# Four one-bank buffers instead of two two-bank buffers for the second product of an attention and MLP kernel

## The chip, the core and the metric

The kernel runs on one core of a Trainium2 chip, as one launch. The metric is the device time of that launch in microseconds (us). Five engines work side by side, each through its own queue in order: TensorE (PE, its weight loads PEld), VectorE (DVE), ScalarE (ACT), GpSimd (POOL), and SyncE (SP), which here issues all DMAs. Results of PE land in PSUM, which has eight banks; a bank holds 512 float32 values in each of 128 partitions.

## The reference

Causal attention by blocks of 64 over 8 batches, 8 heads, 576 positions and head size 64, and behind it a layer norm and an MLP with a residual:

```python
scores = scale * np.matmul(q, k.transpose(0, 1, 3, 2))
scores = np.where(block_i >= block_j, scores, -1000000000.0)
attn = np.exp(scores - np.max(scores, axis=-1, keepdims=True))
attn = attn / (np.sum(attn, axis=-1, keepdims=True) + 1e-09)
x = np.matmul(attn, v)            # then to (8, 576, 512)
...
xn = (x - mu) / np.sqrt(var + 1e-06) * g_ln
ch = np.maximum(xn @ w_ch1, 0.0) @ w_ch2      # 512 -> 2048 -> 512
return x + ch
```

## The kernel before

All work is recorded first as tasks of a plan (`Plan`): each task has an engine (or a choice of engines), an estimated cost, a priority, and buffers that it reads and writes (`Buf`). `Plan.run` walks through an estimated time and gives each engine the ready task of lowest priority number, and this order is the order of the instructions in the engine's queue. A buffer that is made by `kind` takes a slot when its first task is placed and gives it back when its last one ends in that estimate. The waits between engines are not written by hand: a layer below derives them from which instruction touches which tile, so the plan's opinion on when a buffer is free sets the order, and the tile sets the wait.

Attention goes over 32 pairs of heads. `pair` computes scores on PE into PSUM (`scores1` into one-bank buffers `s1`, `scores0` into two buffers `s` of two banks each), `soften` takes them out on DVE and ACT, PE turns the result (`tr`), multiplies it with v (`o`), and DVE turns that and stores it (`xd`). PSUM is divided in two kinds: the tag `tr` has four one-bank slots (`tr`, `s1`, `o`, and later `p`), the tag `s` has two two-bank slots (`s`, and later `y`).

The MLP takes the 36 tiles of 128 rows in six rounds of six. `norm_tiles` loads two tiles at a time (`x<-xd`, L612), scales them (L621), takes their statistics (L630, POOL's L648 to L651), normalises (L656, L659), turns them on DVE (`xnt`, L661) and through DRAM (`xw`, L665, and back as `xt`, L669). `operands` makes from `xt` the seven operands `xm` of a Strassen product, each as a high and a low part (L218, L686, L697). Of round n+1 all this runs beside the products of round n.

In each round there are eight groups. `products` computes the hidden units of a group with seven products `p` of six matmuls each (L789); ACT and DVE take them out (L797, L802) and make the ReLU in two parts, `h` (L808, L809). `second` is the second matrix product, one group later: for each of the six tiles of the round a **y block** of six matmuls of 512 columns (L852) goes into one PSUM bank, and DVE adds that bank to the running sum of the tile in SBUF, `ya` (L861). In PE's queue the steps of a group stand as p, y, p, y, p, p, y, p, y, p, y, y, p, by the priorities in `second` and `products`: called in the text the first to sixth y block of a group.

Two two-bank buffers, `yb2`, are made once and are held through the whole MLP; block number m uses half m modulo 4 of the four halves. `owner` remembers which block used a half last, and the plan makes a block wait for the sum that read the block four before it:

```python
yb, old = yb2[at_y // 2], owner.get(at_y)
hold = 512 * (at_y % 2)
...
add("PE", 6 * (512 / 2400 + MMO), go, ..., w=[part, *([old] if old else [])], alloc=[yb], ...)
```

Of the kernel before, what the change touches and what calls it, by code (L numbers as in the profile page):

```python
# [9 lines left out]
F32 = mybir.dt.float32  # L10
# [6 lines left out]
PSUM = bass.MemoryType.PSUM  # L17

P = 128
# [6 lines left out]
MMO = .0134  # L26
# [30 lines left out]
class Plan:  # L57
# [5 lines left out]
    def add(self, eng, cost=None, fn=None, r=(), w=(), prio=0.0, size=0, alloc=(), mode=128):  # L63
        k = Task(eng if isinstance(eng, dict) else {eng: (cost, fn)}, prio, size)
        k.mode = mode
        before = {}
        for x in r:
            before.update(dict.fromkeys(x.writers))
        for x in w:
            before.update(dict.fromkeys(x.readers))  # L70
        for x in r:
            x.readers.append(k)
        for x in w:
            x.writers.append(k)
        for x in before:
            x.next.append(k)
        k.left = len(before)
        k.uses = list(dict.fromkeys(x.root for x in (*r, *w, *alloc)))
        for x in k.uses:
            x.users += 1  # L80
        k.allocs = [x for x in dict.fromkeys(x.root for x in (*w, *alloc)) if x.make]
        self.tasks.append(k)
        return k
# [88 lines left out]
def dve(n):  # L172
    return .07 + n / 960
# [10 lines left out]
def attn_mlp_kernel(ctx: ExitStack, tc: tile.TileContext, qk, qk0, v, v0, w1, w2, g, out):  # L184
# [8 lines left out]
    nc = tc.nc  # L193
    NPAIR, _, _, S = qk.shape
# [8 lines left out]
    psum = ctx.enter_context(tc.tile_pool(name="psum", bufs=1, space=PSUM))  # L203
    odd = ctx.enter_context(tc.tile_pool(name="odd", bufs=1))
    plan = Plan()
    add = plan.add
# [15 lines left out]
    def kind(name, shape, dtype, bufs, space=None, tag=None, most=None):  # L222

        tag = tag or name
        plan.free.setdefault(tag, bufs)
        own = (tag, "of " + name) if most else (tag,)
        if most:
            plan.free["of " + name] = most

        def make():  # L230
            return (space or sb).tile(shape, dtype, name=name, tag=tag, bufs=bufs)

        def new():
            x = Buf(own, make)
            if space is not dram and name not in ("tr", "s1", "o"):
                x.after, last[name] = [y for y in (last.get(name),) if y], x
            return x
        return new


    new_s, new_y2 = (kind(n, [P, 1024], F32, 2, psum, "s") for n in ("s", "y"))
    steps = {}
    new_tr, new_s1, new_o, new_p = (kind(n, [P, 512], F32, 4, psum, "tr") for n in ("tr", "s1", "o", "p"))

# [52 lines left out]
    def load(nbytes, fn, **kw):  # L297
        add("SP", .6, fn, size=nbytes, **kw)
# [3 lines left out]
    w2b, w1b = {}, {}  # L302

    def decode(j, second, prio, gate):
        n = 512
        wrb, magb, sgnb = new_word(), new_mag(), new_sgn()
# [48 lines left out]
    def pe(at, phase, *args, **kw):  # L355
        steps.setdefault((at, phase), []).append(add("PE", *args, **kw))

    ends, big_of, batch_sums = {}, {}, {}

    def pair(k):  # L360
        b, c = k // 4, k % 4
        prio = 100 + 10 * k
        step = [0]

        def pr():
            step[0] += 1
            return prio + .05 * step[0]
# [23 lines left out]
        def soften(p, s, nm, at, i, h, cols):  # L391

            n = cols.stop - cols.start
            low, x, m = Buf(parent=p), Buf(parent=p), Buf(parent=nm)
            hide = never[:, 576 - n:576] if h else never[:, 512:512 + n]
            add("DVE", dve(n) + .01, lambda: nc.vector.tensor_tensor_reduce(  # L396
                out=p.t[:, part(i, h)], in0=s.t[:, cols], in1=hide, scale=-0.125, scalar=3e38, op0=ALU.add, op1=ALU.min,
                accum_out=nm.t[:, at:at + 1]), r=[s], w=[low, m], prio=pr())
            add("ACT", act(n, True) + .14, lambda: nc.scalar.activation(  # L399
                out=p.t[:, part(i, h)], in_=p.t[:, part(i, h)], func=AF.Exp, bias=nm.t[:, at:at + 1], scale=-1.0,  # L400
                accum_out=totals[:, i - 1, h:h + 1]), r=[low, m], w=[x, sums], prio=pr())
            return x
# [43 lines left out]
        done = [[], []]  # L446
        for h, s in enumerate(sab):
            for n, (i, cols) in enumerate(((4, slice(0, 576)), (3, slice(576, 1024)))):
                done[h].append(soften(pab, s, nm, 2 * h + n, i, h, cols))
        pt0 = big_of[k, 1] = new_pt0()  # L450
        got = []

        for h in range(2):
            for i in (4, 3):
# [4 lines left out]
                else:  # L459
# [5 lines left out]
                     r=[o], w=[x], prio=pr())  # L465
# [9 lines left out]
        for h in range(2):  # L475
# [12 lines left out]
            r=[v_sb, *got], w=[part_o[1]], alloc=[ot], prio=pr(), mode=1)  # L488
# [86 lines left out]
    for k in range(NPAIR):  # L575
        pair(k)
        if k % 8 == 3:
            first(k // 8)
    plan.chain([x for at in sorted(steps) for x in steps[at]])

    n = 0
    for j in range(NJ):
        for second in (False, True):
            decode(j, second, 100 + 10 * (D_0 + D_1 * n), [ends[min(int(D_0 + D_1 * n) - 3, NPAIR - 1)]])
            n += 1
# [244 lines left out]
        return {k: (hs[k], v) for k, v in done.items()}  # L830

    acc = {}
    yb2, owner, turn_y = [new_y2(), new_y2()], {}, [0]

    def second(n, gp, hs, base):

        for pair_, (s0, s1) in enumerate(((3, 4), (5, 0), (1, 2))):
            for z, s in enumerate((s0, s1)):
                at_y = turn_y[0] % 4
                turn_y[0] += 1  # L840
                yb, old = yb2[at_y // 2], owner.get(at_y)
                hold = 512 * (at_y % 2)
                t, h, at = ROUND * n + s, s // HALF_R, s % HALF_R * P
                part = owner[at_y] = Buf(parent=yb)

                def go(hold=hold, h=h, at=at, yb=yb):
                    y = yb.t[:, hold:hold + 512]
                    for i in range(2):
                        j = 2 * gp + i
                        x, (wh, wl) = hs[i, h][0], w2s[j // 4]  # L850
                        for e, (l, w) in enumerate(((0, wh), (0, wl), (1, wh))):
                            nc.tensor.matmul(y, x.t[:, l, at:at + P], w.t[:, j % 4], start=i == e == 0, stop=i == 1 and e == 2)  # L852
                add("PE", 6 * (512 / 2400 + MMO), go, r=[*hs[0, h][1], *hs[1, h][1], *w2b[2 * gp], *w2b[2 * gp + 1]], w=[part, *([old] if old else [])],
                    alloc=[yb], prio=base + (7, 21, 37, 51, 65, 75)[2 * pair_ + z])
                if gp == 0:
                    ya = new_ya()
                    load(P * 2048, lambda t=t, ya=ya: nc.sync.dma_start(out=ya.t, in_=xrow[t].t), r=[xparts_t[t]], w=[ya], prio=4)
                    acc[t] = ya, ya
                ya, was_ = acc[t]
                now = Buf(parent=ya)  # L860
                add("DVE", dve(512), lambda hold=hold, yb=yb, ya=ya: nc.vector.tensor_add(  # L861
                    ya.t, yb.t[:, hold:hold + 512], ya.t), r=[part, was_], w=[now], prio=1)
                acc[t] = ya, now
                if gp == GROUPS - 1:
                    load(P * 2048, lambda t=t, ya=ya: nc.sync.dma_start(out=out[t], in_=ya.t), r=[now], w=[], prio=2)
# [3 lines left out]
    for n in range(ROUNDS):  # L869
        for q in range(HALF_R):  # L870
            norm_tiles(n, q, 100 + 10 * LN_0 + q if n == 0 else END + 2 * n - 10, gate)
        operands(n, 100 + 10 * LN_0 + 3 if n == 0 else 2)
        for gp in range(GROUPS):
            base = 1e6 + 100 * (GROUPS * n + gp)
            hs = products(n, gp, base)
            if gp == 0:
                gate = hs[0, 0][1]
            if before:
                second(*before, base)
            before = n, gp, hs  # L880
# [5 lines left out]
def _run_one(arrays):  # L886
    import numpy as np
    import concourse.bacc as bacc
    from concourse.bass_utils import run_bass_kernel_spmd

    nc = bacc.Bacc("TRN2", target_bir_lowering=False, num_devices=1, dynamic_dma_scratch_size=1024)
    args = {n: nc.dram_tensor(n, a.shape, mybir.dt.from_np(a.dtype), kind="ExternalInput").ap()
            for n, a in arrays.items()}
    for n in ("w1", "w2"):
        args[n] = args[n].bitcast(I32)
    args["out"] = nc.dram_tensor("out_t", (36, P, 512), F32, kind="ExternalOutput").ap()
    with tile.TileContext(nc) as tc:
        attn_mlp_kernel(tc, *args.values())
    r = run_bass_kernel_spmd(nc, [arrays], core_ids=[0])
    return np.asarray(r.results[0]["out_t"])  # L900
# [37 lines left out]
```

## Time and profile before

| what | value |
|---|---|
| median of 3 runs | 1136.12 us (1132.82 to 1141.36) |
| the profiled execution | 1135.29 us |
| its span, first to last instruction | 1133.5 us |
| TensorE clock granted over the span | 0.992 of full speed |
| PE busy | 1075.6 us, 95% of the span |
| DVE busy | 802.6 us, 71% |
| ACT busy | 463.1 us, 41% |
| POOL busy | 270.3 us, 24% |

The profile comes from one execution of its own, 1135.29 us long; 1.8 us of it lie outside the span. A matmul is shown with an end that is modelled and reaches into the next one, so PE's busy time is not its work at full pace, and a stretch in which PE lost time may still show it as busy. The first y block starts 333.9 us after the start of the span, the last sum at 1129.6 us; what lies between is the MLP, what lies ahead is attention, with the first groups of the MLP woven in from 317.5 us on.

### The profile page before, as it was taken

Reading aid. Unit: us, or ns where it says so; the run is one execution under the profiler, and the core shown is the slowest. Engines: PE = TensorE matmul, PEld = TensorE weight load, DVE = VectorE, ACT = ScalarE, POOL = GpSimd, SP = SyncE. Lnnn points to the kernel's source line nnn. Section 1 sums busy time; section 2 is a strip of 40 time slices with the busy share of each in tenths; the row PEclk is TensorE's granted clock in tenths of the full one; section 3 lists DMA queues with packets and bytes.
Section 4 is the critical chain, followed back from the end, with each engine's and each line's share of the span. In section 5 each row is a group of like instructions: output and inputs, shape, how many; then the busy total and the mean of one; then the engine's idle time right before and its main releaser. Section 6 shows DMA issues by size and latency. Waiting matters only on the chain.

```text
span 1133.5 us, 18643 instructions
## 1 busy us (share of the span) xinstructions
PE 1075.6 (95%) x6576; PEld 903.7 (80%) x6576; DVE 802.6 (71%) x1801; ACT 463.1 (41%) x1152; POOL 270.3 (24%) x426
## 2 busy tenths in 40 slices
PE   9999998999988898899999999999999899999998
PEld 6777666777777787788888888887888788888887
DVE  5878987888798888666676565866667666754544
ACT  6778878898853332212132122322223122322221
POOL 0013725322366642112221121212201122100000
PEclk9999999999999999999999999999999999999999
DMA  5559786956587746767637765387645776363311
GB/s 177 156 164 264 228 238 233 268 206 213 190 312 248 228 142 213 220 176 193 182 125 241 190 191 167 114 240 205 177 149 178 207 197 173 137 211 123 125 71 56
DMA packets 232173, 213.31 MB, mean 188 GB/s; under 512 B 158736, under 2 KB 187408, under 8 KB 225936
## 3 DMA queue, kind: packets, MB, share of 16 engines
q1 hardware_dynamic: 232080, 212.12, 61.2%
q8 instruction: 52, 0.85, 0.3%
q14 instruction: 41, 0.34, 0.1%
HBM read 155.45 MB, written 56.62 MB: 187 GB/s over the span
## 4 chain that ended last, share of the span: by engine, by line
PE 59%; DVE 19%; DMA 8%; SPq 5%; ACT 3%; issue 3%; POOL 2%; DVEq 0%; POOLq 0%; ACTq 0%
PE y L852 26%; PE p L789 19%; PE s L381 4%; PE tr L408 4%; PE o L418 4%; DVE ya L861 3%; DMA x<-xd 3%; DMA wr<-w 3%; SPq L612 2%; PE o L414 2%; DMA ya<-xrow 2%; DVE h L809 2%; ACT pu L399 1%; DVE pab L396 1%; DVE xm L697 1%
## 5 line engine op out<-in xcount | busy, mean ns | idle before, releaser
L852 PE MATMUL y<-w2h,h 128*128 128x512 f32 x1152 | 402.4, 398 | 31.4 <-DVE ya L861 31.2
L861 DVE TENSOR_TENSOR ya<-y,ya 128x512 f32<-128x512 f32 x288 | 196.8, 685 | 193.7 <-PE y L852 187.7
L852 PEld LDWEIGHTS y<-w2h,h 128*128 128x128 f32 x1152 | 217.1, 188 | 85.3 <-DVE ya L861 42.3
L789 PE MATMUL p<-xm,wa 128*128 128x384 f32 x1152 | 226.8, 339 | 3.3 <-DVE xm L697 1.7
L852 PE MATMUL y<-w2l,h 128*128 128x512 f32 x576 | 227.5, 395 | 0.0
L789 PEld LDWEIGHTS p<-xm,wa 128*128 128x128 f32 x1152 | 207.2, 190 | 12.1 <-DVE xm L218 2.0
L808 ACT ACTIVATE h<-t 128x384 fp32r<-128x384 f32 x144 | 75.6, 525 | 328.6 <-DVE t L802 325.5
L789 PE MATMUL p<-xm,wb 128*128 128x384 f32 x864 | 177.1, 340 | 2.8 <-ACT t L797 2.4
L789 PEld LDWEIGHTS p<-xm,wb 128*128 128x128 f32 x864 | 156.5, 189 | 15.2 <-ACT t L797 2.7
L852 PEld LDWEIGHTS y<-w2l,h 128*128 128x128 f32 x576 | 108.8, 189 | 15.8
L797 ACT COPY t<-p 128x384 f32<-128x384 f32 x144 | 68.5, 476 | 112.0 <-PE p L789 105.7
L802 DVE TENSOR_TENSOR t<-p,t 128x384 f32<-128x384 f32 x144 | 79.2, 550 | 26.7 <-PE p L789 26.5
L381 PE MATMUL s<-raw 64*128 64x320 f32 (+4 forms) x640 | 96.8, 439 | 1.3 <-DMA raw<-qk 0.6
L809 DVE SCALAR_TENSOR_TENSOR h<-t,h 128x384 fp32r<-128x384 f32 x144 | 83.2, 578 | 16.8 <-ACT h L808 16.2
L399 ACT ACTIVATE pab<-pab,nm 128x576 f32<-128x576 f32 (+1 forms) x128 | 91.4, 726 | 4.2 <-DVE nm L396 4.0
L381 PEld LDWEIGHTS s<-raw 64*128 64x128 f32 x640 | 61.7, 189 | 37.3 <-issue 29.3
L396 DVE CUSTOM_DVE_ANT_0 pab<-s,never 128x576 f32<-128x576 f32 (+1 forms) x128 | 82.9, 684 | 3.6 <-PE s L381 3.1
L418 PE MATMUL o<-pt,v 128*64 128x256 f32 (+1 forms) x768 | 81.0, 346 | 0.0
L418 PEld LDWEIGHTS o<-pt,v 128*64 128x64 f32 x768 | 56.9, 138 | 26.8 <-issue 0.8
L408 PE MATMUL tr<-ident,pab 128*128 128x128 f32 x512 | 67.6, 278 | 11.1 <-ACT pt L216 6.0
L399 ACT ACTIVATE pu<-pu,nm 128x320 f32<-128x320 f32 (+1 forms) x128 | 64.1, 504 | 29.0 <-DVE nm L396 27.6
L686 POOL TENSOR_TENSOR tt<-xt 128x256 f32<-128x256 f32 x21 | 16.0, 761 | 250.1 <-DVE xm L697 130.2
(91 smaller groups left out, 1130.9 us busy)
## 6 DMA issues: line engine op xcount, KB each, us to landing
wa<-was SPq DMA_DIRECT2D x40, 1024.0 KB, 5.2
wb<-wbs SPq DMA_DIRECT2D x40, 768.0 KB, 4.4
raw<-qk SPq DMA_DIRECT2D x32, 576.0 KB, 4.3
wr<-w SPq DMA_DIRECT2D x32, 512.0 KB, 6.4
v<-v SPq DMA_DIRECT2D x32, 320.0 KB, 4.3
x<-xd SPq DMA_DIRECT2D x144, 64.0 KB, 3.1
xrow<-x SPq DMA_DIRECT2D x36, 256.0 KB, 4.7
xw<-xnt SPq DMA_DIRECT2D x144, 64.0 KB, 3.6
```

The source lines that it names most:

```text
L381: nc.tensor.matmul(x, raw.t[HALF[h], 0, col], raw.t[HALF[h], 1, at:at + x.shape[1]], start=True, stop=True)
L396: add("DVE", dve(n) + .01, lambda: nc.vector.tensor_tensor_reduce(out=p.t[:, part(i, h)], in0=s.t[:, cols], in1=hide, scale=-0.125, scalar ...
L399: add("ACT", act(n, True) + .14, lambda: nc.scalar.activation(out=p.t[:, part(i, h)], in_=p.t[:, part(i, h)], func=AF.Exp, bias=nm.t[:, at ...
L408: nc.tensor.transpose(o.t[:, n * P:(n + 1) * P], x, ident)
L418: nc.tensor.matmul(o.t[HALF[h], at + lo:at + 256], v_sb.t[:, ck, HALF[h]], rhs(h), start=False, stop=(n == len(steps) - 1), skip_group_che ...
L789: nc.tensor.matmul(x.t[:, 0:TN], w_(l), xs[m].t[:, :, o, k], start=start and k == e == 0, stop=k == 1 and e == 2, skip_group_check=True)
L797: add("ACT", act(TN), lambda: nc.scalar.copy(out=t.t, in_=x.t[:, 0:TN]), r=[r], w=[new], prio=0)
L802: add("DVE", dve(TN), lambda: nc.vector.tensor_add(t.t, x.t[:, 0:TN], t.t), r=r, w=[new], prio=0)
L808: add("ACT", act(TN, True), lambda: nc.scalar.activation(out=x.t[:, 0, 0:TN], in_=src(), func=AF.Relu), r=r, w=[hi], prio=0)
L809: add("DVE", dve(TN), lambda: nc.vector.scalar_tensor_tensor(out=x.t[:, 1, 0:TN], in0=src(), scalar=0.0, in1=x.t[:, 0, 0:TN], op0=ALU.max, ...
L852: nc.tensor.matmul(y, x.t[:, l, at:at + P], w.t[:, j % 4], start=i == e == 0, stop=i == 1 and e == 2)
L861: add("DVE", dve(512), lambda hold=hold, yb=yb, ya=ya: nc.vector.tensor_add(ya.t, yb.t[:, hold:hold + 512], ya.t), r=[part, was_], w=[now] ...
```

## The change

The score buffers `s` get a PSUM pool of their own, `banks`. When the first y block is placed, that pool is closed and another, `banks_y`, is opened in its place with four slots of one bank. Each y block makes a buffer of its own there (`new_y()`), 288 in all, in place of a half of one of two lasting buffers; it gives the slot back when its sum is done. `owner`, `turn_y` and `hold` go away. Since the banks are those of the scores, each block is also told to come after the last four `soften` results of the last pair (`final`). Matmuls, sums, their sizes and their priorities stay as they are.

```diff
-    new_s, new_y2 = (kind(n, [P, 1024], F32, 2, psum, "s") for n in ("s", "y"))
+    banks = tc.tile_pool(name="banks", bufs=1, space=PSUM)
+    new_s = kind("s", [P, 1024], F32, 2, banks.__enter__())
+    class Again:
+        pool = None
+        def tile(self, *args, **kw):
+            if self.pool is None:
+                banks.__exit__(None, None, None)
+                self.pool = ctx.enter_context(tc.tile_pool(name="banks_y", bufs=1, space=PSUM))
+            return self.pool.tile(*args, **kw)
+    new_y = kind("y", [P, 512], F32, 4, Again())
...
+        final[k] = [*done[0], *done[1]]
...
-    yb2, owner, turn_y = [new_y2(), new_y2()], {}, [0]
...
-                at_y = turn_y[0] % 4
-                turn_y[0] += 1
-                yb, old = yb2[at_y // 2], owner.get(at_y)
-                hold = 512 * (at_y % 2)
+                yb = new_y()
...
-                    y = yb.t[:, hold:hold + 512]
+                    y = yb.t
...
-                add("PE", ..., r=[*hs[0, h][1], ...], w=[part, *([old] if old else [])],
+                add("PE", ..., r=[*final[NPAIR - 1], *hs[0, h][1], ...], w=[part],
                     alloc=[yb], prio=base + (7, 21, 37, 51, 65, 75)[2 * pair_ + z])
...
-                add("DVE", dve(512), lambda hold=hold, yb=yb, ya=ya: nc.vector.tensor_add(
-                    ya.t, yb.t[:, hold:hold + 512], ya.t), r=[part, was_], w=[now], prio=1)
+                add("DVE", dve(512), lambda yb=yb, ya=ya: nc.vector.tensor_add(
+                    ya.t, yb.t, ya.t), r=[part, was_], w=[now], prio=1)
```

On every engine the order of attention stands as it was, up to about the place where the first products of the MLP begin. From there on three places matter. Line numbers from L356 on are 10 to 14 higher in the changed kernel: L789, L802, L809, L852 and L861 become L803, L816, L823, L862 and L871.

The first place is PE in the first group of round 2 (rounds are counted from 0). Here stand the last matmul of the group's first y block, the next product, and the beginning of the second y block. Before:

```order
L852 MATMUL y_4220<-w2h0_1385,h_6738 128x512 [waits DVE_49]
L789 MATMUL p_6783<-xm4_1396,wa_6538 128x384 x6
L852 MATMUL y_4220<-w2h0_1385,h_6718 128x512 [waits DVE_49]
L852 MATMUL y_4220<-w2l0_1391,h_6718 128x512
L852 MATMUL y_4220<-w2h0_1385,h_6718 128x512
```

Now:

```order
L862 MATMUL y_6869<-w2h0_1388,h_6827 128x512 [waits DVE_49]
L803 MATMUL p_6881<-xm4_1399,wa_6714 128x384 x6
L862 MATMUL y_6892<-w2h0_1388,h_6806 128x512
L862 MATMUL y_6892<-w2l0_1394,h_6806 128x512
L862 MATMUL y_6892<-w2h0_1388,h_6806 128x512
```

The order is the same. Two neighbouring blocks wrote the same two-bank buffer (y_4220), and the second began with a wait for DVE; now each has a buffer of its own, and that wait is not there.

The second place is DVE at the same time, where the sums of the two neighbouring blocks before these stand (the fifth and sixth y block of a group). Before:

```order
L861 TENSOR_TENSOR ya_6651<-y_4168,ya_6651 128x512 [waits DMAHW0_49,PE_49]
L809 SCALAR_TENSOR_TENSOR h_6738<-t_6649,h_6738 128x384 [waits Activation_49]
L661 STREAM_TRANSPOSE xnt_6749<-x_6540 128x512 [waits Pool_49]
L861 TENSOR_TENSOR ya_6666<-y_4168,ya_6666 128x512 [waits DMAHW2_49]
L809 SCALAR_TENSOR_TENSOR h_6767<-p_6604,h_6767 128x384 [waits Activation_49]
```

Now:

```order
L871 TENSOR_TENSOR ya_6743<-y_6816,ya_6743 128x512 [waits DMAHW7_49,PE_49]
L823 SCALAR_TENSOR_TENSOR h_6827<-t_6752,h_6827 128x384 [waits Activation_49]
L871 TENSOR_TENSOR ya_6754<-y_6829,ya_6754 128x512 [waits DMAHW0_49,PE_49]
L670 TENSOR_SCALAR x_6642<-x_6642,norm_6727 128x512 [waits DMAHW6_49,Pool_49]
L823 SCALAR_TENSOR_TENSOR h_6866<-p_6703,h_6866 128x384 [waits Activation_49]
```

Both sums read the same buffer y_4168, and only the first of them waited for PE; now each waits for PE itself. The normalising steps between them moved by a few rows.

The third place is PE at the border of round 0 and round 1, where the first product of round 1 (on xm0) begins. Before:

```order
L852 MATMUL y_4220<-w2h3_4218,h_5305 128x512
L789 MATMUL p_5376<-xm0_1393,wa_5063 128x384 [waits DMAHW3_49,DVE_49]
L789 MATMUL p_5376<-xm0_1393,wa_5063 128x384 [waits DVE_49]
L789 MATMUL p_5376<-xm0_1393,wa_5063 128x384 x4
L789 MATMUL p_5387<-xm4_1396,wa_5063 128x384 [waits DVE_49] x2
```

Now:

```order
L803 MATMUL p_5186<-xm3_1576,wb_5193 128x384 [waits Pool_49]
L803 MATMUL p_5186<-xm3_1576,wb_5193 128x384 x3
L803 MATMUL p_5356<-xm0_1396,wa_5119 128x384 [waits DMAHW4_49,Activation_49]
L803 MATMUL p_5356<-xm0_1396,wa_5119 128x384 [waits Pool_49]
L803 MATMUL p_5356<-xm0_1396,wa_5119 128x384 x4
L862 MATMUL y_5374<-w2h3_4213,h_5306 128x512
```

All six y blocks of round 0's last group stood ahead of the first product of round 1; now they stand behind it and between the products that follow, as at the other borders of rounds. On DVE the last turning step of round 1's rows (L661) stood behind 41 sums, and stands behind 37 now; the other rounds keep their pattern, with steps shifted by a few rows.

## Rows read from the trace of the kernel before

**Rows 1.** Head of the page: span, busy time and share of PE and others.

```profile
span 1133.5 us, 18643 instructions
...
PE 1075.6 (95%) x6576; PEld 903.7 (80%) x6576; DVE 802.6 (71%) x1801; ACT 463.1 (41%) x1152; POOL 270.3 (24%) x426
```

**Rows 2.** Costliest groups: busy us, mean ns | idle before, what ended it.

```profile
L852 PE MATMUL y<-w2h,h 128*128 128x512 f32 x1152 | 402.4, 398 | 31.4 <-DVE ya L861 31.2
```

**Rows 3.** PE's waits in 334 to 470, 470 to 1000: us, times, longest.

```profile
PE y L852 <- DVE ya L861: 12.8, 10, 1.8
...
PE y L852 <- DVE ya L861: 18.4, 20, 1.9
```

**Rows 4.** Timeline of PE around 640 us: start, us, what, [idle before].

```profile
637.54 1.21 PE L789 MATMUL p<-xm,wb 128*128 128x384 f32 x6
640.59 0.50 PE L852 MATMUL y<-w2h,h 128*128 128x512 f32 x1 [1.84 <-DVE ya L861]
```

**Rows 5.** Timeline of DVE at the same time.

```profile
639.24 0.69 DVE L621 TENSOR_TENSOR x<-x,sums_all 128x512 f32<-128x512 f32 x1 [2.16 <-DMA x<-xd]
639.85 0.68 DVE L861 TENSOR_TENSOR ya<-y,ya 128x512 f32<-128x512 f32 x1
```

**Rows 6.** Short windows: busy of PE, PEld, DVE, ACT, POOL; granted clock, DMA.

```profile
355.50:358.50 3.00, 3.00 (x10) 2.71 (x9) 1.59 (x6) 0.00 (x0) 0.32 (x2) 0.50 0.82 240
471.50:474.50 3.00, 3.00 (x11) 3.00 (x10) 3.00 (x10) 0.88 (x2) 0.15 (x1) 0.50 0.95 358
642.30:646.00 3.70, 3.70 (x13) 3.32 (x12) 1.71 (x3) 0.58 (x2) 0.00 (x0) 0.57 1.01 229
888.30:891.20 2.90, 2.90 (x9) 2.42 (x8) 2.48 (x3) 0.37 (x1) 1.28 (x1) 0.50 0.60 249
```

**Rows 7.** The MLP by stretches, columns as in Rows 6.

```profile
334.00:470.00 136.00, 121.05 (x573) 104.34 (x571) 110.93 (x202) 40.83 (x84) 63.35 (x86) 0.99 0.67 206
470.00:600.00 130.00, 123.39 (x603) 109.81 (x604) 89.56 (x181) 32.84 (x72) 24.80 (x53) 0.99 0.61 176
600.00:730.00 130.00, 126.13 (x613) 111.33 (x613) 85.96 (x168) 30.70 (x68) 23.92 (x52) 0.99 0.62 182
730.00:860.00 130.00, 126.21 (x621) 111.17 (x620) 86.55 (x172) 31.13 (x69) 24.71 (x53) 1.00 0.65 186
860.00:990.00 130.00, 124.15 (x603) 109.07 (x602) 84.84 (x167) 29.89 (x65) 21.93 (x50) 0.99 0.64 187
990.00:1128.00 138.00, 138.00 (x683) 122.88 (x682) 70.71 (x123) 29.57 (x63) 2.89 (x4) 1.00 0.32 113
```

**Rows 8.** Timeline: end of two neighbouring blocks on PE, first sum on DVE.

```profile
457.77 0.39 PE L852 MATMUL y<-w2h,h 128*128 128x512 f32 x1
...
458.19 0.69 DVE L861 TENSOR_TENSOR ya<-y,ya 128x512 f32<-128x512 f32 x1 [1.74 <-PE y L852]
```

**Rows 9.** The chain that ended last, its end: start, us, what.

```profile
1113.43 1.05 PE p L789 x6
...
1120.73 8.21 PE y L852 x36
...
1128.97 0.69 DVE ya L861
```

**Rows 10.** Two lines of DVE: shortest, median, longest in ns.

```profile
L861 DVE TENSOR_TENSOR ya<-y,ya x288: 645/691/693, 337.1 to 1129.6; 128x512 f32<-128x512 f32 x144
...
L759 DVE TENSOR_TENSOR wa<-sum,wa x8: 676/714/1765, 316.7 to 421.6; 128x512 fp32r<-128x512 f32 x8
```

**Rows 11.** Border of rounds 0 and 1: DVE's timeline, the chain, PE's timeline.

```profile
459.27 0.71 DVE L661 STREAM_TRANSPOSE xnt<-x 128x512 f32<-128x512 f32 x1
...
466.63 3.65 DMA xt<-xw
...
469.00 0.44 PE L789 MATMUL p<-xm,wa 128*128 128x384 f32 x1 [1.58 <-DVE xm L218]
471.12 1.14 PE L789 MATMUL p<-xm,wa 128*128 128x384 f32 x3 [1.67 <-DVE xm L697]
```

More of the change, by code (lines that the diff above doesn't have):

```diff
@@ L356, in pe @@
         steps.setdefault((at, phase), []).append(add("PE", *args, **kw))
-    ends, big_of, batch_sums = {}, {}, {}
+    ends, big_of, batch_sums, final = {}, {}, {}, {}
     def pair(k):
@@ L838, in second, with go @@
             for z, s in enumerate((s0, s1)):
-                at_y = turn_y[0] % 4
-                turn_y[0] += 1
-                yb, old = yb2[at_y // 2], owner.get(at_y)
-                hold = 512 * (at_y % 2)
+                yb = new_y()
                 t, h, at = ROUND * n + s, s // HALF_R, s % HALF_R * P
-                part = owner[at_y] = Buf(parent=yb)
-                def go(hold=hold, h=h, at=at, yb=yb):
-                    y = yb.t[:, hold:hold + 512]
+                part = Buf(parent=yb)
+                def go( h=h, at=at, yb=yb):
+                    y = yb.t
                     for i in range(2):
@@ L852, in go @@
                             nc.tensor.matmul(y, x.t[:, l, at:at + P], w.t[:, j % 4], start=i == e == 0, stop=i == 1 and e == 2)
-                add("PE", 6 * (512 / 2400 + MMO), go, r=[*hs[0, h][1], *hs[1, h][1], *w2b[2 * gp], *w2b[2 * gp + 1]], w=[part, *([old] if old else [])],
+                add("PE", 6 * (512 / 2400 + MMO), go, r=[*final[NPAIR - 1], *hs[0, h][1], *hs[1, h][1], *w2b[2 * gp], *w2b[2 * gp + 1]], w=[part],
                     alloc=[yb], prio=base + (7, 21, 37, 51, 65, 75)[2 * pair_ + z])
```

## The prediction

> **What bounds the kernel now.** I read the head of the page first: PE is busy for 95% of the span [rows 1], so PE's queue sets the time, and the only thing to win is time in which PE stands still or runs at a lower clock. The costliest groups name the one large stop: ahead of the y blocks' first matmuls PE is idle for 31.4 us, and 31.2 of it ends with DVE's sum L861 [rows 2]. PE's waits put it in time: 12.8 us in 10 waits in round 0 (334 to 470 us), 18.4 us in 20 waits from there to 1000 us, none above 1.9 us [rows 3]. The split by stretches agrees: PE is short of a full stretch by 15 us in 334 to 470, by 4 to 7 us in each of the next four, by nothing in the last, in which no rows are normalised any more [rows 7].
>
> One of these waits shows the mechanism. PE's queue stands from the end of a product until 640.59 [rows 4]. DVE had waited 2.16 us for a load of `x`, scaled it at 639.24, and made the sum at 639.85 [rows 5]; PE's block begins when that sum ends, at 640.54. What the block waits for is the sum of the y block just ahead of it, not of the one four before, whose half it overwrites. The two neighbours write two halves of one two-bank buffer, and the wait goes by the buffer. So on the second and fourth block of a group, DVE has only the time of one product between, 1.05 us [rows 9], to begin and end a sum of 0.69 us [rows 10]: any load, statistic or operand step that stands ahead of the sum in DVE's queue stops PE.
>
> The same tie holds the other way. The fifth and sixth block stand next to each other, and the sum of the fifth begins at 458.19, after 1.74 us of idle DVE, once the last matmul of the sixth (from 457.77) is done [rows 8], though its own bank was full a block earlier, some 1.4 us.
>
> **The change part by part.** The 1,728 matmuls, 288 sums, weight loads, output stores and banks (four before, four after) are as before, so nothing is added to any engine's work.
>
> The wait for the neighbour goes. In rounds 1 to 4 PE's idle time is 18.4 us. Each wait costs more than it shows: the six products from 637.54 issue in 1.05 us [rows 9], so the next matmul was due at 638.59 and came at 640.59; 2.00 us were lost where 1.84 are shown [rows 4]. I add 0.16 to each of the 20: 18.4 + 3.2 = 21.6 us.
>
> Some waits also lower PE's clock. Behind three of them the granted clock is at its lower level, 1.2 GHz in place of 2.4, wholly or for most of a short window: 3.0 us at 0.50, 3.7 at 0.57 and 2.9 at 0.50 [rows 6]; what PE did before each was a wait of over 1.8 us. Lost work is length times (1 - clock): 1.5 us in round 0, and 1.6 + 1.45 = 3.0 in the rounds behind. (The fourth window, at 471.5, follows a wait for operands and is not the change's.)
>
> Round 0 has 12.8 + 10 x 0.16 = 14.4 us of lost issue, and 1.5 of clock: 15.9 us. Here it is less sure that PE can use what it gets. DVE is busy for 110.9 of the 136 us [rows 7]; with 15.9 us less it would be 110.9 of 120.1, 92%, in a queue in strict order that also waits for POOL and loads. Bounds are 0 and 15.9. I take three quarters, 12: DVE is given back idle time too (the 1.74 us of rows 8 happens once in each group), but 92% is above every other stretch.
>
> In rounds 1 to 4 DVE's share is 65 to 69% [rows 7], and I take the whole. A sum that is late by two microseconds now matters only if it is late by four blocks. What is late next is the last product of a group, which waits until DVE has emptied the bank it adds to: two y blocks, 2 x 1.37 = 2.7 us [rows 9], lie between that bank's filling and its next use, against one DVE step of about 0.55 us. And the first y block of the next group needs the last `h`. These have more slack than the 1.05 us that go, but not four blocks; a burst of DVE work can still reach PE there. Nothing in the trace shows its price apart from the waits that go; between 0 and some 5 us (a quarter of the 18.4) I take 2.
>
> At the end, the last two sums stand one behind the other after the last matmul: the last block ends near 1128.95, the sums start at 1128.97 and 1129.6 [rows 9, 10]. The first of the two can now run beside the last block: 0.6 us.
>
> The border of rounds 0 and 1 has another order. Before, six y blocks (8.21 us by the six at the end [rows 9]) ran ahead of round 1's first product, and PE still lost time there: 1.58 us, 1.67 us [rows 11], and 1.5 us of clock [rows 6], for operands whose way from the turning step at 459.27 through DRAM ended with a load of 3.65 us and gave the second matmul at 471.12: 11.85 us [rows 11]. Now the six blocks stand behind, but the turning step stands behind 37 sums, not 41. From the 38th block to the first product of round 1, PE has 5 y blocks and 5 products, 5 x 1.37 + 5 x 1.05 = 12.1 us. That is just the length of the way, so I expect about the same loss as before and count nothing, with bounds of 5 us won (all of the loss above) and the rivals' price below.
>
> `final` and the second pool: PE's first y block waits for an `h` that comes from products running long after the last `soften`, and its place in the queue is the same, so I count nothing; a gain isn't possible there, and a loss would be one exposed wait like those of rows 4, about 2 us.
>
> Sum: 21.6 + 3.0 + 12 + 0.6 - 2 = 35.2 us less. From the profiled execution's 1135.29 us this gives **1100 us**. The median of the runs is 0.8 us above that execution, which I leave in the rounding.
>
> **A rule that speaks against it.** The waits of rows 4 and 5 end with the neighbour's sum, not with that of four blocks before. The Trainium skill says in "Trainium Kernel Development and Optimization", Best Practices, that consistent bubbles can mean that SBUF or PSUM ran out. By that rule there would be no gain here, since the change adds no bank: 1135 us, the second rival below. The trace speaks against the rule: a pipeline that had run out of four banks would wait for the oldest sum, not the youngest.
>
> **The rivals.** (1) *DVE and the chain of `norm_tiles` pace round 0.* For it: DVE's 82% in 334 to 470 us with POOL at 63 us beside it [rows 7], and a line of DVE whose step takes 714 ns mostly but 1765 ns once [rows 10]. Against it: DVE's idle waits for PE in the same stretch. If the operands of round 1 give the second matmul at 471.1 us as before, everything behind it takes what it took (1135.3 - 471.1 = 664.2), less 24.6 and 0.6 for the later rounds and the end, plus the 8.2 us of six y blocks that now stand behind: 471.1 + 664.2 - 25.2 + 8.2 = 1118 us. With half the hindrance it is 1110 or so. On the slow step, the Trainium skill's "SBUF — State Buffer", Who interferes with whom, says that a DVE instruction with two SBUF inputs and a GpSimd instruction that reads SBUF hold a port pair in turn, each for its whole length; the sums, with one input in PSUM, would be spared, and they do stay within 645 to 693 ns [rows 10]. By that rule POOL's steps go on stretching DVE's in round 0 however PE is freed, and the time is this rival's 1118 us.
>
> (2) *The time stays.* The neighbour's wait is only the first place where PE meets a late DVE; each lateness comes back in full at the last product or at `h`. Then only the end's 0.6 us are won: 1135 us. For it: DVE is one queue, and those two waits stand in every group. Against it: DVE idles for 30% and more in rounds 1 to 4, so it catches up.
>
> (3) *Slower.* The operands of round 1 come late, with no y blocks ahead of the first product to cover it. SP's queue issues the `x`, `xw` and `xt` transfers and the weight loads in strict order, its order has changed there, and a waiting `xw` store holds the loads behind it. By the sum of rival 1, the total is 1118 us when the second matmul comes at 471.1, and a microsecond more for each one later; it is slower than before from 488 us on, with say 490 us: 1137, and slower by 1% from 500. Against it: DVE's turning step moved four sums earlier, not later.
>
> **How the numbers follow.** Forecast (1090 to 1110) 0.70; rival 1 (1110 to 1124) 0.17; rival 2, with rests of rival 1 above 1124: 0.09; rival 3: 0.04. About 1% is what a measurement of this kernel tells from no change: 1125 and 1147 us. Faster 0.87, same 0.10, slower 0.03 (a fourth of rival 3 stays within 1%). Lowest is all of it: 21.6 + 3.0 + 15.9 + 0.6 and the border's 5, 46 us, 1089 us. The range leaves out rivals 2 and 3 and a little at either end: 1090 to 1119 us.
>
> **What would show it.** In the profile of the changed kernel: (a) PE's wait at the y blocks for the sum falls from 31.2 us to under 5. (b) DVE's idle wait of 1.7 us before the sum of the fifth block is gone, and two neighbours' sums are a block apart. (c) 470 to 990 us hold no window at half clock behind a y block's wait. (d) The first matmul of round 1 starts near 449 us: 469 less 12 and 8.2. If it starts near 470, rival 1 holds; beyond 488, rival 3. (e) If PE's waits at the products (L803) grow to over 10 us, rival 2 has come in. The forecast is wrong if PE's idle time in 334 to 1000 us falls by less than 25 us.

## The result, and the profile after

The changed kernel takes 1103.64 us (median of 4 runs, 1101.26 to 1107.53) against 1134.47 us for the kernel before (1130.69 to 1141.36): a ratio of 0.9725, with an interval of 0.9668 to 0.9782. The prediction was 1100 us, in 1090 to 1119. Its profiled execution took 1102.45 us, 32.8 less than the one of before, and the spans differ by as much (1133.5 and 1100.7).

The head of the page of the changed kernel, the lines that answer to [rows 1]:

```profile
span 1100.7 us, 18673 instructions
...
PE 1065.7 (97%) x6576; PEld 902.7 (82%) x6576; DVE 804.1 (73%) x1797; ACT 464.0 (42%) x1154; POOL 275.2 (25%) x428
```

PE's busy time fell too, by 10 us, with the same 6,576 matmuls: the ends of matmuls are modelled, and part of what was lost stood in "busy". The groups that answer to [rows 2] (busy us, mean ns | idle before, what ended it), the y blocks first, now and before in [rows 2]; then the products on `wb`, to which the seventh of a group belongs, before (L789) and now (L803); then the sums, before (L861) and now (L871):

```profile
L862 PE MATMUL y<-w2h,h 128*128 128x512 f32 x1152 | 398.8, 394 | 0.0
...
L789 PE MATMUL p<-xm,wb 128*128 128x384 f32 x864 | 177.1, 340 | 2.8 <-ACT t L797 2.4
...
L803 PE MATMUL p<-xm,wb 128*128 128x384 f32 x864 | 176.6, 339 | 17.3 <-DVE t L816 12.9
...
L861 DVE TENSOR_TENSOR ya<-y,ya 128x512 f32<-128x512 f32 x288 | 196.8, 685 | 193.7 <-PE y L852 187.7
...
L871 DVE TENSOR_TENSOR ya<-y,ya 128x512 f32<-128x512 f32 x288 | 197.0, 684 | 115.2 <-PE y L862 114.9
```

The 31.2 us at the y blocks are gone to the last tenth. A part is back in another place: at the products, where 2.8 us of idle time stood before, PE now waits 17.3 us. In the waits of PE from 334 us to the end (us, times, longest), this is all that is left of the MLP's waits for other engines' work (14.7 us; in the kernel before it was 34.9 with the 31.2 for sums), and it answers to [rows 3]:

```profile
PE p L803 <- DVE t L816: 10.7, 9, 1.8
PE p L803 <- ACT t L811: 4.0, 2, 3.7
```

One of the nine waits for DVE's L816, in the timelines of PE and DVE, with the window behind it (columns as in [rows 6]; the row of PE shows four of the product's six matmuls):

```profile
527.23 0.96 PE L803 MATMUL p<-xm,wb 128*128 128x384 f32 x4 [1.79 <-DVE t L816]
...
524.76 0.70 DVE L644 BATCH_NORM_STATS2 st<-x 128x6 f32<-128x512 f32 x1 [3.84 <-DMA x<-xd]
...
526.63 0.55 DVE L816 TENSOR_TENSOR t<-p,t 128x384 f32<-128x384 f32 x1
...
528.70:532.00 3.30, 3.30 (x11) 2.96 (x11) 2.38 (x7) 0.94 (x2) 1.99 (x10) 0.54 0.77 321
```

It is the story of [rows 4, 5] at the next place where PE meets DVE. DVE waits 3.84 us for a load of `x`; the sums behind it are late, but PE has four banks and goes on through two y blocks; then comes the seventh product of the group, which adds to a bank that DVE's L816 must have read, and PE stands 1.79 us. The granted clock is 0.54 over the 3.3 us behind, so the lower level for most of them.

Where the time came from is read off the starts of y blocks in PE's timeline: the first of all, the first of round 1, the first of round 5; and of what PE does next after the last product of round 0, where the border begins. Before (the border's row is the second; the 333.9 us given ahead for the first block is the start of its weight load):

```profile
334.11 0.39 PE L852 MATMUL y<-w2h,h 128*128 128x512 f32 x1
...
459.06 0.39 PE L852 MATMUL y<-w2h,h 128*128 128x512 f32 x1
...
481.99 0.39 PE L852 MATMUL y<-w2h,h 128*128 128x512 f32 x1
...
1011.86 0.39 PE L852 MATMUL y<-w2h,h 128*128 128x512 f32 x1
```

After (the border now begins with round 1's first product):

```profile
332.88 0.63 PE L862 MATMUL y<-w2h,h 128*128 128x512 f32 x1
...
447.93 0.34 PE L803 MATMUL p<-xm,wa 128*128 128x384 f32 x1
...
464.74 0.39 PE L862 MATMUL y<-w2h,h 128*128 128x512 f32 x1
...
980.19 0.39 PE L862 MATMUL y<-w2h,h 128*128 128x512 f32 x1
```

Round 0 with its border took 147.9 us and takes 131.9, 16.0 less: 9.9 up to the end of its last product (125.0 and 115.1), 6.1 at the border (22.9 and 16.8). Rounds 1 to 4 took 529.9 and take 515.5, 14.4 less. Round 5 and the end took 121.6 (to the span's 1133.5) and take 120.5, 1.1 less. The rest, 1.2 us, lies ahead of the first y block. Sum 32.8 before rounding.

At the end, the chain that ended last has the answer to [rows 9]:

```profile
1088.79 8.22 PE y L862 x36
...
1097.03 0.69 DVE ya L871
```

The six blocks are the same, but only one sum comes after them, where before two did: the span ends 3.7 us after this last sum's start, where before it ended 4.5 us after the chain's first sum began. DVE's timeline shows the last two sums a block apart (1.36 us), each behind its own block:

```profile
1095.67 0.69 DVE L871 TENSOR_TENSOR ya<-y,ya 128x512 f32<-128x512 f32 x1 [0.67 <-PE y L862]
1097.03 0.69 DVE L871 TENSOR_TENSOR ya<-y,ya 128x512 f32<-128x512 f32 x1 [0.67 <-PE y L862]
```

### The profile page after: what moved, and what is told of

It reads as the page before. It is cut to its first block, busy times and chain, and to the rows that moved or that the text cites. A ratio compares the mean times of both kernels' runs of the same rounds, so it can differ in the third digit from the quotient of the medians.

```text
span 1100.7 us, 18673 instructions
## 1 busy us (share of the span) xinstructions
PE 1065.7 (97%) x6576; PEld 902.7 (82%) x6576; DVE 804.1 (73%) x1797; ACT 464.0 (42%) x1154; POOL 275.2 (25%) x428
## 4 chain that ended last, share of the span: by engine, by line
PE 56%; DVE 20%; DMA 9%; SPq 4%; issue 4%; ACT 3%; POOL 2%; DVEq 0%; POOLq 0%; ACTq 0%
PE y L862 21%; PE p L803 20%; PE s L394 4%; PE o L431 4%; PE tr L421 4%; DMA xt<-xw 3%; DMA x<-xd 3%; DVE ya L871 3%; DVE xm L711 2%; PE o L427 2%; DVE h L823 2%; DVE t L816 2%; DVE pab L409 2%; SPq L679 1%; DVE x L670 1%
## 5 line engine op out<-in xcount | busy, mean ns | idle before, releaser
L862 PE MATMUL y<-w2h,h 128*128 128x512 f32 x1152 | 398.8, 394 | 0.0
L871 DVE TENSOR_TENSOR ya<-y,ya 128x512 f32<-128x512 f32 x288 | 197.0, 684 | 115.2 <-PE y L862 114.9
L862 PEld LDWEIGHTS y<-w2h,h 128*128 128x128 f32 x1152 | 217.7, 189 | 39.1
L862 PE MATMUL y<-w2l,h 128*128 128x512 f32 x576 | 228.2, 396 | 0.0
L803 PE MATMUL p<-xm,wa 128*128 128x384 f32 x1152 | 225.4, 337 | 0.6 <-DVE ot L504 0.6
L803 PEld LDWEIGHTS p<-xm,wa 128*128 128x128 f32 x1152 | 205.3, 189 | 9.6 <-DVE ot L504 0.9
L803 PE MATMUL p<-xm,wb 128*128 128x384 f32 x864 | 176.6, 339 | 17.3 <-DVE t L816 12.9
L803 PEld LDWEIGHTS p<-xm,wb 128*128 128x128 f32 x864 | 153.6, 188 | 35.2 <-DVE t L816 19.3
L862 PEld LDWEIGHTS y<-w2l,h 128*128 128x128 f32 x576 | 108.7, 189 | 15.9
L823 DVE SCALAR_TENSOR_TENSOR h<-t,h 128x384 fp32r<-128x384 f32 x144 | 81.9, 569 | 22.0 <-ACT h L822 21.9
L816 DVE TENSOR_TENSOR t<-p,t 128x384 f32<-128x384 f32 x144 | 79.1, 550 | 21.4 <-PE p L803 20.9
L662 POOL TENSOR_TENSOR norm<-norm 128x2 f32<-128x2 f32 x54 | 12.4, 229 | 254.5 <-DVE norm L656 251.6
```

The costliest lines, as they stand in the source:

```text
L803: nc.tensor.matmul(x.t[:, 0:TN], w_(l), xs[m].t[:, :, o, k], start=start and k == e == 0, stop=k == 1 and e == 2, skip_group_check=True)
L816: add("DVE", dve(TN), lambda: nc.vector.tensor_add(t.t, x.t[:, 0:TN], t.t), r=r, w=[new], prio=0)
L823: add("DVE", dve(TN), lambda: nc.vector.scalar_tensor_tensor(out=x.t[:, 1, 0:TN], in0=src(), scalar=0.0, in1=x.t[:, 0, 0:TN], op0=ALU.max, ...
L871: add("DVE", dve(512), lambda yb=yb, ya=ya: nc.vector.tensor_add(ya.t, yb.t, ya.t), r=[part, was_], w=[now], prio=1)
```

## The experiments

All ratios are to the kernel before, as it was measured beside each run, with 95% intervals. The last two columns are us in the profiled execution, from 334 us on.

| run | time, us | ratio | PE's waits for sums in the MLP | PE's waits for DVE's L802 (in its line there), at the products |
|---|---|---|---|---|
| kernel before | 1134.47 | 1 | 31.2 | 0.4 |
| changed kernel | 1103.64 | 0.9725 (0.9668 to 0.9782) | 0 | 10.7 |
| own_banks_old_order | 1107.9 | 0.9773 (0.9728 to 0.9819) | 0 | 16.6 |
| tied_banks_new_order | 1129.8 | 0.9965 (0.9938 to 0.9993) | 31.3 | 1.7 |
| neighbours_apart | 1112.05 | 0.9793 (0.9743 to 0.9843) | 15.2 | 0 |
| two_buffers | 1104.72 | 0.9736 (0.9699 to 0.9773) | 12.0 | 0 |
| all_four_tied | 1147.99 | 1.0112 (1.0066 to 1.0158) | 43.7 | 0 |
| last_product_later | 1088.99 | 0.9605 (0.9567 to 0.9642) | 0 | 0 |
| last_product_104 | 1085.26 | 0.9560 (0.9535 to 0.9585) | 0 | 0.6 |
| last_product_later_tied | 1122.93 | 0.9894 (0.9857 to 0.9930) | 24.5 | 0 |

The question is whether the waits or the order made the gain, since the change altered both: the planner, with other buffers to hand out, put round 0 and its border in another order.

**own_banks_old_order.** The kernel before, with the two lasting buffers made of two one-bank tiles each; the planner still sees two buffers of two banks, and every instruction on every engine stands where it stood.

```diff
-    new_s, new_y2 = (kind(n, [P, 1024], F32, 2, psum, "s") for n in ("s", "y"))
+    banks = tc.tile_pool(name="banks", bufs=1, space=PSUM)
+    new_s = kind("s", [P, 1024], F32, 2, banks.__enter__())
+    class Two:
+        def __init__(self, tiles):
+            self.tiles = tiles
+        def __getitem__(self, at):
+            return self.tiles[at[1].start // 512]
...
+            return Two([self.pool.tile([P, 512], dtype, name=..., tag=..., bufs=1) for k in range(2)])
+    new_y2 = kind("y", [P, 1024], F32, 2, Again(), "s")
```

> The kernel before with one edit: each of the two lasting two-bank buffers of the MLP becomes two one-bank buffers, and the plan is not told. Every instruction of every engine stands in the order of the kernel before; only the waits between PE and DVE at the y blocks are those of the changed kernel (four blocks back). Theory of the tie (two neighbours in one buffer): the waits alone are the gain, 1100 to 1112 us, and PE's wait at y blocks for sums goes from 31 us to under 2. Rival, the order (the planner's new order from round 0 on, with the border of rounds 0 and 1, is the gain): 1130 to 1138 us.

Measured 1107.9 us, ratio 0.9773. In its waits of PE from 334 us on, no sum stands any more, and the products have taken over more than in the changed kernel (L810 and L823 are this kernel's L789 and L802):

```profile
PE p L810 <- DVE t L823: 16.6, 12, 2.9
PE p L810 <- ACT t L818: 3.6, 2, 2.9
PE p L810 <- DVE xm L718: 1.6, 1, 1.6
PE p L810 <- DVE xm L218: 1.0, 1, 1.0
```

The waits alone give 2.3% of the 2.75%. In the profiled executions the share is smaller: from the first y block to the end this kernel took 778.2 us, the kernel before 799.4, the changed kernel 767.8, so 21.2 of 31.6 us. The last two rows are the border of rounds 0 and 1, which still loses time in the old order, as in [rows 11].

**tied_banks_new_order.** The other corner: the order of the changed kernel, instruction for instruction, with neighbours tied again.

```diff
-        pool = None
+        pool, made, two = None, 0, []
...
-            return self.pool.tile(*args, **kw)
+                self.two = [self.pool.tile([P, 1024], F32, name=f"yy{k}", tag=f"yy{k}", bufs=1) for k in range(2)]
+            at, self.made = self.made % 4, self.made + 1
+            return self.two[at // 2][:, 512 * (at % 2):512 * (at % 2) + 512]
```

> The changed kernel with one edit: the four slots are halves of two lasting two-bank buffers, so neighbours are tied again; every instruction of every engine stands in the order of the changed kernel. Theory of the tie: the waits come back, 30 to 40 us at the y blocks, 1125 to 1142 us. Rival, the order: 1100 to 1108 us.

Measured 1129.8 us, ratio 0.9965, and 797.7 us in the profiled execution from the first y block to the end. The waits are back, in PE's waits from 334 us on (`yy` are the two tiles of this kernel):

```profile
PE yy L864 <- DVE ya L873: 31.3, 29, 2.6
```

So with the tie as it was, the new order is worth 0.35%, and with the tie gone 0.5% (0.9773 to 0.9725, within each other's intervals). By the medians the tie is worth 2.3 to 2.4% in either order, and the rival, that the order is the gain, is out.

**neighbours_apart.** Two lasting two-bank buffers as before, and no new pool; only who shares is changed.

```diff
-                yb, old = yb2[at_y // 2], owner.get(at_y)
-                hold = 512 * (at_y % 2)
+                yb, old = yb2[at_y % 2], owner.get(at_y)
+                hold = 512 * (at_y // 2)
```

> The kernel before, still with two lasting two-bank buffers, but neighbouring y blocks use different buffers (block m uses buffer m modulo 2), so that the tie is to the block two before; order as before. Theory of the tie: a block then waits for a sum that has a y block and one or two products more time, 2.4 us or more instead of 1.05, and most of the 31 us go: 1100 to 1118 us. Rival, that the size of the buffer or the pool of its own matters and not who shares it: 1130 to 1138 us.

Measured 1112.05 us, ratio 0.9793. PE's waits for sums, over the MLP:

```profile
PE y L852 <- DVE ya L861: 15.2, 19, 2.2
```

Half of the waits went with two changed lines, and most of the gain came with them (2.1 of 2.75%), within the intervals of the 2.3% of own_banks_old_order, which has the same order. So what a block shares its buffer with decides; no further gain from smaller buffers or a pool of their own shows.

**two_buffers.** The changed kernel with half the banks; the order of the instructions stays that of the changed kernel.

```diff
-    new_y = kind("y", [P, 512], F32, 4, Again())
+    new_y = kind("y", [P, 512], F32, 2, Again())
```

> The changed kernel with two one-bank buffers for the y blocks in place of four; a block waits for the sum two before, as with neighbours apart in two two-bank buffers. Theory of the tie: half the banks cost a few us only, 1104 to 1116 us. Rival, that the waits of the kernel before meant too few banks: as slow as before or slower, 1130 us and more.

Measured 1104.72 us, ratio 0.9736, with four banks 0.9725, within each other's intervals. A block waits for the sum two before, as in neighbours_apart, and PE's waits for sums are much the same:

```profile
PE y L862 <- DVE ya L871: 12.0, 13, 1.9
```

So the kernel before had no lack of banks, and that rival is out: two untied banks do what four do. Of the 13 waits 11 stand at the sixth y block, just ahead of the seventh product, and the seventh product then waits for L816 no more: 12.0 us for sums in place of 10.7 at the product.

**all_four_tied.** The tie widened: all four slots in one four-bank buffer, the order as in the changed kernel. Shown against tied_banks_new_order:

```diff
-                self.two = [self.pool.tile([P, 1024], F32, name=f"yy{k}", tag=f"yy{k}", bufs=1) for k in range(2)]
+                self.two = [self.pool.tile([P, 2048], F32, name="yy", tag="yy", bufs=1)]
...
-            return self.two[at // 2][:, 512 * (at % 2):512 * (at % 2) + 512]
+            return self.two[0][:, 512 * at:512 * at + 512]
```

> The changed kernel with one edit: the four slots are quarters of one lasting four-bank buffer, so a y block is tied to the one just ahead in five places of a group instead of two; order of all instructions as in the changed kernel. Theory of the tie: each such place has about 0.1 us of room when DVE is on time, and twice or three times the waits come, 60 to 100 us, 1155 to 1195 us. Rival, that a late DVE is caught up with in one wait and further ties cost nothing: 1128 to 1140 us.

Measured 1147.99 us, ratio 1.0112: slower than with neighbours tied, as the theory has it, but by 18 us and not by the 25 to 65 that I expected. PE's waits for sums in the MLP:

```profile
PE yy L864 <- DVE ya L873: 43.7, 60, 2.5
```

Twice the waits (60 against 29), but each is shorter (0.7 us against 1.1). At the second and fourth y block, the only ones that waited with neighbours tied, 31.3 us became 21.6, and the other four blocks have 22.1. I read this as the rival's idea in part: one wait lets DVE catch up, and the next tie finds it less late. But further ties do cost something, which the rival denied.

**last_product_later** and **last_product_104.** The changed kernel, with the seventh product of a group moved behind the next group's first product (104), or behind its first y block too (110). Shown for 110:

```diff
-        p4 = product(4, a, False, [p7], [p7], 90)
+        p4 = product(4, a, False, [p7], [p7], 110)
```

> The changed kernel with the seventh product of a group (the one that waits 12.9 us for DVE) at 110 in place of 90, that is behind the next group's first product and first y block, 2.4 us later. If that wait is DVE's lateness against too little room: the 12.9 us and the clock lost behind them go, 1086 to 1097 us. Rival, that DVE's lateness only moves to the next wait (the sums four blocks back, or h): 1098 to 1108 us. If the bank that it holds longer becomes short for the next group's products: slower than 1108 us.

> The changed kernel with the seventh product at 104: behind the next group's first product (1.05 us later), ahead of its first y block. Half of the room that 110 gives. If the wait is a matter of room: most of the 12.9 us go, 1088 to 1098 us.

Measured 1088.99 (110) and 1085.26 us (104), ratios 0.9605 and 0.9560: 15 and 18 us below the changed kernel, the best of this study, and for 104 also 3 us below the range expected. One product more of room, 1.05 us, is enough; the second step gains nothing more. For 110, PE's waits of the MLP are down to these four, all in round 0 and at its border, and the stretches behind show PE without a gap at full clock where [rows 7] had gaps of 4 to 7 us (one of them, columns as there):

```profile
PE p L803 <- DVE xm L711: 3.3, 1, 3.3
PE p L803 <- ACT t L811: 1.7, 1, 1.7
PE p L803 <- DVE xm L218: 1.0, 1, 1.0
PE y L862 <- DVE h L823: 0.5, 1, 0.5
...
600.00:730.00 130.00, 130.00 (x649) 116.91 (x648) 93.52 (x180) 32.59 (x70) 26.68 (x54) 1.00 0.65 190
```

The edit moves more than the one product: from the first moved product on, the planner also put steps of DVE, ACT, POOL and the loads in another order. That PE's waits for L816 went, the trace shows; how much of the 15 to 18 us is the room and how much the new order, no run separates.

**last_product_later_tied.** The same line (110) in the kernel before.

> The kernel before (neighbours tied) with the seventh product of a group at 110 in place of 90. Theory of the tie: in the kernel before, this product hardly waits (0.4 us), since the waits for sums hold PE back first; so nothing to gain, 1126 to 1138 us. Rival, that the later product is a gain by itself, whatever the banks: 15 us less, 1115 to 1122 us.

Measured 1122.93 us, ratio 0.9894: a gain of 12 us where I expected none; the rival said about 15, in 1115 to 1122 us. The waits of PE for sums, in 334 to 470 and in 470 to 1000 us, against [rows 3]:

```profile
PE y L852 <- DVE ya L861: 13.0, 7, 3.2
...
PE y L852 <- DVE ya L861: 11.6, 14, 2.5
```

In round 0 the waits are as they were; in the later rounds 18.4 us became 11.6. My expectation looked at the seventh product's own wait alone and missed where the product went: it now stands between the next group's first and second y block, so that tied pair has two products between it, 2.1 us, instead of one. By its starts in PE's queue, the second block of a group had 13 of the waits before, and has one here. The fourth block has 20 waits in place of 17. So part of the gain is the theory of the tie again, which I had not seen ahead; the 6.8 us less of waits are not all of the 12, and what the new order of the other engines adds is not shown.

## Why the prediction was right, and where it was off

*The mechanism* was right where the gain comes from. The wait was for the neighbour's sum in the shared buffer; it went altogether (31.2 to 0 us; point (a) said under 5), and the two crossed kernels, with equal order and unequal tie, show that it made 83 to 87% of the gain by the medians (2.27 and 2.40 of 2.75%), and 21.2 and 29.9 of the 31.6 us by which the MLP shrank in the profiled executions. The other side of the tie went too (point (b)): DVE's idle time before the sums fell from 193.7 to 115.2 us, and the last sum stands alone at the end.

*The clock.* No window at half clock follows a y block any more (point (c)). Two in the MLP follow the products' waits (at 378 us, behind one of 3.7 us for ACT, and at 528 us, above), which I had not counted.

*Round 0 and the border.* Counted 12 + 0, came 9.9 + 6.1. The border did not lose its 4.8 us again: the first product of round 1 began at 447.93 (point (d): near 449), and it and the next ran without a wait. That is a little over the upper bound that I named for the border. Round 0 itself gave 9.9 of its 15.9, below the three quarters that I took, so the 12 came right only because the border made up for it. What is missing in round 0 stands at the products again: 3.7 us for ACT's copy, 1.2 for L816, and 1.7 for the 3.8 us at a clock of 0.55 from 378 on. That copy of ACT had itself waited 2.50 us for DVE:

```profile
376.62 0.48 ACT L811 COPY t<-p 128x384 f32<-128x384 f32 x1 [2.50 <-DVE wb L773]
```

The first rival (DVE and the chain pace round 0, start near 470) is out; so is the third, since the operands were there.

*Rounds 1 to 4: the term that was mis-sized.* I counted 24.6 less 2 for new waits; 14.4 came. The mis-sized term is the 2 us for "a burst of DVE work can still reach PE there", with 5 us as its bound. In 450 to 1000 us PE waits 9.5 us in 7 waits for L816; with 0.16 for each and 1.5 us for the window at 0.54 that is 12.1 us, six times the term and beyond its bound. I had held the two y blocks' 2.7 us of room against one DVE step of 0.55 us, as if DVE came to that step on time. But the old waits had held PE back to a late DVE in up to two places of each group, so the trace of before could not show how late DVE gets when PE doesn't wait; a load for which DVE waits 3.84 us is passed on to the next place that needs DVE, as 1.79 us of PE. In own_banks_old_order it is more still, 16.6 us. last_product_later gives a measure from the other side: PE runs three of its rounds, from the first y block of round 2 to that of round 5, without a wait, each in 125.12 us:

```profile
587.06 0.39 PE L862 MATMUL y<-w2h,h 128*128 128x512 f32 x1
...
712.18 0.39 PE L862 MATMUL y<-w2h,h 128*128 128x512 f32 x1
...
837.30 0.39 PE L862 MATMUL y<-w2h,h 128*128 128x512 f32 x1
...
962.42 0.39 PE L862 MATMUL y<-w2h,h 128*128 128x512 f32 x1
```

Four such rounds are 500.5 us. The kernel before took 29.4 us more for rounds 1 to 4, the changed kernel 15.0 more. So the 24.6 was too small by 4.8 and the 2 by 13, and the first error hides part of the second. The second rival (all lateness comes back) was thus right for about half of those rounds. Point (e) set its mark at 10 us, and the products' waits are at 14.7: by that mark the second rival has come in, though not with its time of 1135 us, since about half of the lateness did not come back.

*The last mark failed.* I wrote that the forecast is wrong if PE's idle time in 334 to 1000 us falls by less than 25 us. It fell from 35.1 to 15.1, by 20.0 (us, then PE's busy us, and the columns of [rows 7]; before, then now):

```profile
334.00:1000.00 666.00, 630.93 (x3057) 554.60 (x3056) 465.91 (x901) 168.78 (x364) 161.60 (x297) 0.99 0.63 187
334.00:1000.00 666.00, 650.90 (x3210) 580.23 (x3209) 479.75 (x922) 174.26 (x377) 164.65 (x299) 0.99 0.65 196
```

So by its own mark the forecast had the idle time wrong, again by the term for new waits; the time came near all the same, because time that the page counts as busy went too (10 us over the span, above).

That the total came within 4 us of 1100 owes much to chance: 8 us less in the later rounds, 4 more in round 0 and its border, 0.5 more at the end and 1.2 ahead of the first y block. The 1.2 are not the change's gain: up to about 317 us both programs have the same instructions in the same order, and the first product of the MLP already began 2.6 us sooner (314.9 and 317.5); behind it, where the order differs, 1.4 of these were lost again.

*One reason was wrong.* I wrote that the first y block of the next group needs the last `h`. With the seventh product behind that block (110) it runs all the same: the first three blocks need other halves of `h`, and the last one only from the fourth on. That is why the product could be moved at all.

*The rule on bubbles* named a lack of PSUM as what such stops can mean. Here it was none: two_buffers has half the banks and the same time. The stops came from who shared a buffer, not from how many there were.

*The rule on the port pair* foretold the first rival's 1118 us, and the time is 1103.64; DVE's steps do still stretch in round 0 (the changed kernel's L773 for `wa`, eight steps with the same input shapes, takes 678 to 1209 ns), but they no longer reach PE through the sums. No run here takes POOL's work away, so how much of round 0's rest is due to it stays open.

## What to carry to other kernels

Where waits are derived from tiles, give each PSUM bank that is written and read by itself a tile of its own, or at least put neighbours in time into different tiles: two swapped indices gave 2%. A tie that holds the faster engine back also hides how late the slower one is; when the tie goes, look for the next place where the two meet, and give that some room in the same change (here one priority, with what the planner moved behind it, was worth half of the first gain again). And where a change alters both order and waits, build the two crossed kernels, old order with new waits and new order with old waits: they cost one edit each and tell the shares.

## What was not expected of the hardware

The same instructions in the same order took different times ahead of the MLP. The first y block began at 334.1 us in the kernel before, at 333.5 in neighbours_apart and at 330.6 in own_banks_old_order, which have the same order throughout. The ten profiled executions fall in two groups. In five, PE waited 1.83 to 3.56 us for ACT's L216 shortly before 175 us, the granted clock behind it was 0.50, and the first product of the MLP began at 314.9 to 318.0 us. In the other five the wait there was 0.48 to 1.79 us, the clock stayed at 1.00, and that product began at 311.4 to 313.2. One of each, the kernel before and own_banks_old_order (PE's timeline, then the window 174.5 to 176.5 with PE's busy time alone, clock and DMA):

```profile
173.93 1.59 PE L408 MATMUL tr<-ident,pab 128*128 128x128 f32 x8 [3.12 <-ACT pt L216]
174.50:176.50 2.00, 2.00 (x11) 0.50 0.69 275
...
170.52 1.14 PE L429 MATMUL tr<-ident,pab 128*128 128x128 f32 x8 [0.48 <-ACT pt L216]
174.50:176.50 2.00, 2.00 (x20) 1.00 0.01 4
```

Why that wait differs from one execution to the next stays open. A difference of 3 us between two profiles is therefore no sign of a change unless it is found in the stretch that was changed.

Waits of PE a little under two microseconds were followed by the lower clock in some places (1.84 us at 640, with 0.57 behind it, and 1.79 at 527, with 0.54), so that each cost 1.5 to 1.6 us more than itself. It is not the length of the wait alone: in own_banks_old_order PE waited 2.52 us until 531.25, and the granted clock from 531 to 535 us was 1.00.
